# A fused scan and SwiGLU kernel on one core: the input projection of the scan moved next to the gate/up sums, its first loads reordered, its scan steps paced anew

## The chip, the cores and the metric

One core of a Trainium2 chip. The metric is device time in microseconds (us) of one execution. An execution over 1.5% above the fastest one of its kernel counts as slow. The mean granted TensorE clock of a run: 1.0 is full speed.

## The reference, cut to what matters

```python
xn = layernorm(x)                        # x: 2048 x 448, bf16
Bu = xn @ B_bar^T                        # complex, 448 states
h[t] = Lam_bar * h[t-1] + Bu[t]          # over 2048 steps
s  = 2 * Re(h @ C^T) + xn * Dskip
f  = (silu(xn @ w_gate) * (xn @ w_up)) @ w_down     # 448 -> 1792 -> 448
out = x + s * silu(f)
```

## The kernel before

The 2048 tokens are handled in four chunks (q = 0 to 3) of 512. For each chunk TensorE does: the gate/up sums (`gp`, `up`, fourteen tiles of 128 rows, two tiles at a time), the drive of the scan (`pb` six banks, `pk` one bank), the down projection (`hd`, four token tiles) and the output sums (`y`, four token tiles). VectorE turns the drive by a phase (six "E steps" into `ere`, `eim`), runs seven scans, turns back (six "H steps" into `H_re`, `H_im`), multiplies SiLU and up into `Vt`, and finishes each token tile (`t`, `ob`). ScalarE empties the gate/up and drive banks. The scan work is a queue of steps that other work lets through in portions; the budget is roughly VectorE us per call:

```python
def run(self, budget):                       # class Background
    self.credit = min(self.credit + budget, 2.0 * budget)
    while self.steps and self.credit > 0:
        _, cost, fn = self.steps.popleft()
        fn()
        self.credit -= cost
```

The gate/up and pb sums run as 64-row halves on both halves of the array. The second half of such a sum must not start before the first half of the other one is through, and that is told by a notice which passes through GpSimd:

```python
def tell(mm):
    told = nc.gpsimd.nop(nofuse=True)        # waits for mm; the other half waits for it
    tc.add_manual_dep(told.ins, mm.ins.name, SYNC, reason="share")
    return told.ins.name
```

The gate/up sums of a chunk, and what is hung between the pairs of tiles:

```python
def gu(q, bg, budget, hooks={}, begun=None):
    for f0 in range(0, NF, GRP):             # GRP = 4 tiles
        gs = work.tile([P, GRP, W], BF16, name="gs")
        us = work.tile([P, GRP, W], BF16, name="us")
        for i in range(0, n, 2):
            # ... banks gp, up; gu_matmuls; SiLU into gs, copy into us (ScalarE)
            for fn in hooks.get(fi // 2, ()):
                fn()
            bg.run(budget)
        nc.vector.tensor_tensor(out=Vt[...], in0=gs[...], in1=us[...], op=ALU.mult)
```

The order of chunks 1 to 3:

```python
bu_alloc(1)
gu(1, bg, 1.7, {
    0: [on(bu, 1, (0, 1, 2), True), on(bg.run, 5.0)],     # drive after the first pair
    1: [*stats(8, 9), on(ssm_steps, bg, 1)],
    # ... statistics and transposes of the next tokens, C weights
})
for q in range(NQ - 1):
    for j in range(TQ):
        sg.append(down(q, j))
        bg.run(2.2)
        if q + 2 < NQ and j == 1:
            bu(q + 2, (0, 1, 2), True)                    # drive inside the down projection
            bg.run(4.6)
    if q + 2 < NQ:
        ssm_steps(bg, q + 2)
    bg.finish(q)
    for j in range(TQ):
        finish(q, j, out_sum(q, j), sg[j])
    if q + 2 < NQ:
        gu(q + 2, bg, 1.7, {...})
# ... the last chunk
```

## Time and profile before

| | before |
|---|---|
| time, median of 3 runs | 196.47 us (195.99 to 199.16, the last one slow) |
| span of the profiled run, clock | 194.4 us, 0.999 |
| TensorE busy | 185.3 us |
| second tile pair of chunk 0 begins | 13.98 us |
| drive of chunk 1 (pb and pk) | 7.12 us |
| gate/up sums of chunk 2 / of chunk 3 | 23.3 / 21.3 us |

How to read it: TensorE's work sets the length, so what counts are the places where it stands still: the start, the drive of chunk 1, and the start of chunk 2's sums (2 us longer than the same sums of chunk 3). The prediction shows the lines.

### The profile page before, as it was taken

Reading aid. Unit: us, or ns where it says so; the run is one execution under the profiler, and the core shown is the slowest. Engines: PE = TensorE matmul, PEld = TensorE weight load, DVE = VectorE, ACT = ScalarE, POOL = GpSimd, SP = SyncE. Lnnn points to the kernel's source line nnn. Section 1 sums busy time; section 2 is a strip of 40 time slices with the busy share of each in tenths; the row PEclk is TensorE's granted clock in tenths of the full one; section 3 lists DMA queues with packets and bytes.
Section 4 is the critical chain, followed back from the end, with each engine's and each line's share of the span. In section 5 each row is a group of like instructions: output and inputs, shape, how many; then the busy total and the mean of one; then the engine's idle time right before and its main releaser. Section 6 shows DMA issues by size and latency. Waiting matters only on the chain.

```text
span 194.4 us, 3680 instructions
## 1 busy us (share of the span) xinstructions
PE 185.3 (95%) x1463; PEld 94.5 (49%) x1463; DVE 160.3 (82%) x265; ACT 104.3 (54%) x197; POOL 12.0 (6%) x21
## 2 busy tenths in 40 slices
PE   7889999998999999999799999999999999999991
PEld 3465434553444444554357854455444445555550
DVE  4589996799999999999999999998858789780063
ACT  3258699947999944910476751950476754102200
POOL 6322200000002000000003000000000000000000
PEclk9999999999999999999999999999999999999999
DMA  6999998300000240000200400001100000020002
GB/s 155 296 365 389 375 136 177 67 3 2 0 3 0 54 57 2 0 0 3 74 22 18 94 0 0 3 0 47 51 2 0 3 0 0 0 74 24 0 28 68
DMA packets 20977, 12.59 MB, mean 65 GB/s; under 512 B 10976, under 2 KB 19936, under 8 KB 20960
## 3 DMA queue, kind: packets, MB, share of 16 engines
q1 hardware_dynamic: 20544, 12.23, 25.1%
q8 instruction: 11, 0.18, 0.5%
q10 hardware_dynamic: 288, 0.13, 0.3%
q14 instruction: 6, 0.05, 0.1%
q0 software_dynamic: 128, 0.00, 0.0%
HBM read 8.03 MB, written 1.84 MB: 51 GB/s over the span
## 4 chain that ended last, share of the span: by engine, by line
PE 89%; DVE 4%; DMA 3%; SPq 1%; ACT 1%; issue 0%; POOL 0%; DVEq 0%
PE gp L428 23%; PE hd L564 22%; PE up L428 19%; PE y L578 11%; PE pb L428 10%; DMA x_all<-in_A_x_dram 3%; PE pk L451 2%; DVE t L591 2%; PE y L582 2%; DVE ob L593 1%; PE tpb L371 1%; DVE st L230 1%; SPq L144 0%; SPq L183 0%; ACT gs L551 0%
## 5 line engine op out<-in xcount | busy, mean ns | idle before, releaser
L428 PE MATMUL up<-xT,Wu 64*128 64x512 bf16 (+1 forms) x406 | 86.4, 369 | 1.6 <-DVE t L591 1.0
L428 PE MATMUL gp<-xT,Wg 64*128 64x512 bf16 (+1 forms) x406 | 87.0, 369 | 0.4 <-DVE t L591 0.4
L551 ACT ACTIVATE gs<-gp 128x512 bf16<-128x512 f32 x56 | 34.2, 611 | 33.6 <-PE gp L428 30.2
L428 PEld LDWEIGHTS <-Wg 64*128 64x128 bf16 x406 | 37.0, 94 | 24.0 <-issue 3.6
L428 PEld LDWEIGHTS <-Wu 64*128 64x128 bf16 x406 | 37.1, 94 | 19.5 <-POOLq L410 1.3
L564 PE MATMUL hd<-Wd,Vt 128*128 128x448 bf16 x224 | 43.4, 353 | 0.0
L552 ACT ACTIVATE us<-up 128x512 bf16<-128x512 f32 x56 | 34.5, 616 | 0.0
L564 PEld LDWEIGHTS <-Vt 128*128 128x128 bf16 x224 | 21.7, 98 | 21.3 <-issue 0.8
L569 ACT ACTIVATE sg<-hd 128x448 bf16<-128x448 f32 x16 | 8.7, 543 | 29.0 <-PE hd L564 29.0
L591 DVE TENSOR_TENSOR t<-y,sg 128x448 f32<-128x448 f32 x16 | 10.0, 624 | 15.1 <-PE y L578 14.7
L556 DVE TENSOR_TENSOR Vt<-gs,us 128x2048 bf16<-128x2048 bf16 (+1 forms) x16 | 17.3, 1084 | 5.5 <-ACT us L552 5.5
L428 PE MATMUL pb<-xT,BT 64*128 64x512 bf16 x168 | 19.9, 376 | 0.8 <-ACT gs L551 0.7
L578 PE MATMUL y<-C,H_re 128*128 128x448 bf16 x64 | 17.4, 353 | 0.0
L501 DVE TENSOR_TENSOR_SCAN bu_re<-rcol,H_re,ere 128x512 bf16<-128x512 f32 x12 | 15.0, 1266 | 0.0
L428 PEld LDWEIGHTS <-BT 64*128 64x128 bf16 x168 | 8.3, 94 | 11.4 <-issue 2.7
L582 PE MATMUL y<-Dd,xT 128*128 128x128 bf16 x64 | 13.6, 212 | 0.0
L230 DVE BATCH_NORM_STATS2 st<-x_all 128x6 f32<-128x448 bf16 x16 | 9.9, 619 | 3.3 <-DMA x_all<-in_A_x_dram 3.3
L215 POOL TENSOR_TENSOR sd<-vep,halves 128x1 bf16<-128x1 bf16 (+1 forms) x7 | 6.8, 972 | 85.2 <-DVE vep L232 83.2
L578 PE MATMUL y<-C,H_im 128*128 128x448 bf16 x48 | 11.7, 353 | 0.0
L501 DVE TENSOR_TENSOR_SCAN bu_im<-rcol,H_im,eim 128x512 bf16<-128x512 f32 x9 | 11.4, 1261 | 0.0
L463 ACT ACTIVATE bu_re<-pb 128x512 bf16<-128x512 f32 x12 | 7.3, 611 | 6.4 <-PE pb L428 6.4
L593 DVE TENSOR_TENSOR ob<-t,x_all 128x448 bf16<-128x448 f32 x16 | 10.0, 625 | 0.5
(95 smaller groups left out, 174.7 us busy)
## 6 DMA issues: line engine op xcount, KB each, us to landing
out_dram<-ob SPq DMA_DIRECT2D x16, 112.0 KB, 1.7
Wd<-in_B_w_down_dram SPq DMA_DIRECT2D x1, 1568.0 KB, 12.5
x_all<-in_A_x_dram SPq DMA_DIRECT2D x1, 896.0 KB, 14.5
Wg<-in_B_w_gate_dram SPq DMA_DIRECT2D x1, 768.0 KB, 8.2
Wu<-in_B_w_up_dram SPq DMA_DIRECT2D x1, 768.0 KB, 9.2
x_all<-in_A_x_dram SPq DMA_DIRECT2D x1, 448.0 KB, 6.1
Wg<-in_B_w_gate_dram SPq DMA_DIRECT2D x1, 384.0 KB, 6.7
Wu<-in_B_w_up_dram SPq DMA_DIRECT2D x1, 384.0 KB, 5.0
```

The source lines that it names most:

```text
L230: nc.vector.bn_stats(out=st[:], in_=x_all[:, n, :])
L428: mm = nc.tensor.matmul(banks[n][i][:, c0:c1], lhsT=weights[n][i][h, d, :], rhs=xT[h, d, q * W + c0 : q * W + c1], start=(first and m == 0 ...
L501: nc.vector.tensor_tensor_scan(out=T["b"][c][:, k, :], data0=rcol[:, k : k + 1].to_broadcast([P, W]), data1=T["e"][c][:, k, :], initial=in ...
L551: nc.scalar.activation(gs[:, i + j, :], gp_[:], ACT.Silu)
L552: nc.scalar.activation(us[:, i + j, :], up_[:], ACT.Copy)
L556: nc.vector.tensor_tensor(out=Vt[:, f0 : f0 + n, :], in0=gs[:, 0:n, :], in1=us[:, 0:n, :], op=ALU.mult)
L564: nc.tensor.matmul(hd, lhsT=Vt_of[q][:, fi, j * P : (j + 1) * P], rhs=Wd[:, fi, :], start=(fi == 0), stop=(fi == NF - 1),)
L569: nc.scalar.activation(sg[:], hd, ACT.Silu)
L578: nc.tensor.matmul(y, lhsT=h, rhs=C2[:, n, :], start=(n == 0), stop=(n == NS - 1))
L582: nc.tensor.matmul(y[:, s + c0 : s + P], lhsT=xT[:, n, m * P : (m + 1) * P], rhs=Dd[:, n, c0:P], start=False, stop=False,)
L591: nc.vector.tensor_tensor(out=t[:], in0=y, in1=sg[:], op=ALU.mult)
L593: nc.vector.tensor_tensor(out=ob[:], in0=t[:], in1=x_all[:, m, :], op=ALU.add)
```

## The change

The intent: the drive of each chunk becomes one piece beside the gate/up sums, so that TensorE has 5.5 us of other work exactly where it used to wait for banks; the scan steps are let through more slowly during the gate/up sums, so that the late work on VectorE does not stand ahead of `t`; at the start, token tiles 2 and 3 are loaded third, and the transposes of parameters move behind the first half sums.

```diff
-    load_w(nc.sync, nc.scalar, Wg, B_w_gate, 0, C0)
-    load_w(nc.sync, nc.scalar, Wu, B_w_up, 0, C0)
     load_x(2, TQ)
+    load_w(nc.sync, nc.sync, Wg, B_w_gate, 0, C0)
+    load_w(nc.scalar, nc.scalar, Wu, B_w_up, 0, C0)
...
-    nc.scalar.activation(pcol[:], params_row(), ACT.Copy)
-    warm(1)
+    warm(3)
     # statistics of tiles 2, 3; first half sums
...
+    nc.scalar.activation(pcol[:], params_row(), ACT.Copy)
     ln_transpose(2, nc.vector)
...
-    bu_alloc(1)
-    gu(1, bg, 1.7, {
-        0: [on(bu, 1, (0, 1, 2), True), on(bg.run, 5.0)],
-        1: [*stats(8, 9), on(ssm_steps, bg, 1)],
+    gu(1, bg, 0.9, {
+        1: stats(8, 9),
...
+    def drive(q, packed, budget):
+        bu_alloc(q)
+        bu(q, (0, 1, 2), packed)      # pk "first" or "last"
+        ssm_steps(bg, q)
+        bg.run(budget)
+
+    drive(1, "last", 4.8)
     for q in range(NQ - 1):
         for j in range(TQ):
             sg.append(down(q, j))
             bg.run(2.2)
-            if q + 2 < NQ and j == 1:
-                bu(q + 2, (0, 1, 2), True)
-                bg.run(4.6)
...
         if q + 2 < NQ:
+            drive(q + 2, "first", 4.0)
-            gu(q + 2, bg, 1.7, {...})
+            gu(q + 2, bg, 2.2 if last else 1.5, {...})
```

More of the change, by code (lines that the diff above doesn't have):

```diff
@@ L443, in sums, with bu @@
                 between()
-    def bu(q, ns, packed):
+    def bu(q, ns, packed=None):
+        pk = bank("pk") if packed == "first" else None
         pb = [[bank("pb") for _ in range(2)] for _ in ns]
-        pk = bank("pk") if packed else None
+        pk = bank("pk") if packed and pk is None else pk
         def whole():
@@ L456, in bu @@
         pairs = [[BT[:, :, block(n)], BT[:, :, block(KT + n)]] for n in ns]
-        alone = packed and len(ns) == 1
-        sums(pb, pairs, q, 0, W, between=whole if alone else None)
-        if packed and not alone:
+        if packed == "first":
+            whole()
+        sums(pb, pairs, q, 0, W, between=whole if packed == "between" else None)
+        if packed == "last":
             whole()
@@ L659 @@
         2: [*transposes(4, 5, 6, 7), on(load_c), on(table_phase, 1), on(table_sin, 1),
-            on(bu, 0, (0, 1), False), on(table_phase, 2), on(table_sin, 2)],
-        3: [on(bu, 0, (2,), True), on(table_phase, 3), on(table_sin, 3), on(params_fold)],
+            on(bu, 0, (0, 1)), on(table_phase, 2), on(table_sin, 2)],
+        3: [on(bu, 0, (2,), "between"), on(table_phase, 3), on(table_sin, 3), on(params_fold)],
         4: [on(params_trig), on(ssm_steps, bg, 0)],
@@ L673 @@
     })
+    def drive(q, packed, budget):
[4 more added lines that the diff above has]
+    drive(1, "last", 4.8)
     for q in range(NQ - 1):
         sg = []
-        if q + 2 < NQ:
-            bu_alloc(q + 2)
         for j in range(TQ):
@@ L680 @@
             bg.run(2.2)
-            if q + 2 < NQ and j == 1:
-                bu(q + 2, (0, 1, 2), True)
-                bg.run(4.6)
-        if q + 2 < NQ:
-            ssm_steps(bg, q + 2)
         bg.finish(q)
@@ L689 @@
         if q + 2 < NQ:
+            drive(q + 2, "first", 4.0)
             n = (q + 3) * TQ
-            gu(q + 2, bg, 1.7, {
+            last = q + 3 == NQ
+            gu(q + 2, bg, 2.2 if last else 1.5, {} if last else {
                 0: stats(n, n + 1),
@@ L696 @@
                 4: transposes(n + 2, n + 3),
-            } if q + 3 < NQ else {})
+            })
     q = NQ - 1
```

## The prediction

> **What bounds the kernel now.** I read the page's busy shares first, then the busy time by stretch, then the chain of waits around each stretch that fell short, then the order in time of VectorE and the DMA issues there.
>
> ```profile
> PE 185.3 (95%) x1463; PEld 94.5 (49%) x1463; DVE 160.3 (82%) x265; ACT 104.3 (54%) x197; POOL 12.0 (6%) x21
> ...
> PE 89%; DVE 4%; DMA 3%; SPq 1%; ACT 1%; issue 0%; POOL 0%; DVEq 0%
> ```
>
> TensorE is the bound: 185.3 us of 194.4, and 89% of the chain that ended last. A change that keeps its arithmetic can only win back its gaps. The columns below are stretch, length, then busy us and count of PE, PEld, DVE, ACT, POOL, then clock, DMA share, GB/s.
>
> ```profile
> 0.00:14.00 14.00, 11.34 (x109) 6.49 (x111) 8.70 (x34) 4.74 (x8) 5.65 (x17) 1.00 0.88 267
> ...
> 39.00:49.10 10.10, 9.30 (x79) 4.20 (x77) 9.86 (x19) 6.17 (x13) 0.00 (x0) 1.00 0.01 2
> ...
> 89.80:113.10 23.30, 21.86 (x197) 14.13 (x198) 22.38 (x41) 12.99 (x26) 1.92 (x1) 1.00 0.18 43
> ...
> 135.50:156.80 21.30, 21.30 (x198) 9.50 (x198) 16.20 (x16) 13.04 (x26) 0.00 (x0) 1.00 0.04 13
> ```
>
> The gate/up sums of chunk 2 take 23.3 us (89.8 to 113.1), the same sums of chunk 3 only 21.3 (135.5 to 156.8): 2.0 us lost. The other two losses are the start, and the 10 us after 39. The chain at the second:
>
> ```profile
> 42.32 1.74 PE pb L428 x16
> 44.06 0.02 issue
> 44.08 0.60 ACT gs L551
> 44.68 0.50 ACT us L552
> 45.18 0.04 issue
> 45.22 0.80 PE pb L428 x5
> ```
>
> TensorE runs the drive (pb) of chunk 1 after only one pair of gate/up tiles, needs PSUM banks that ScalarE has not emptied, and waits. The SiLU at 44.08 itself waits although its sums ended near 42: its buffer is freed by VectorE's product, which ran late (start, us):
>
> ```profile
> 42.77 1.22 DVE L556 TENSOR_TENSOR Vt<-gs,us 128x2048 bf16<-128x2048 bf16 x1
> ```
>
> At the third, TensorE waits for VectorE to read the y banks:
>
> ```profile
> 90.53 0.21 PE gp L428
> 90.77 0.63 DVE t L591
> 91.42 0.64 DVE ob L593
> ...
> 95.01 0.64 DVE t L591
> 95.69 0.37 PE up L428
> ```
>
> The first y was complete at about 85.2, but VectorE was still in the scan and the H products of chunk 1, queued ahead of t, until 90.8. At the start, token tiles 2 and 3 (issued at 2.66) land at 7.92, where the chain begins that ends in their transposes at 11.21; the weight tiles queued before them land sooner than their first user can run:
>
> ```profile
> 2.66 5.24 DMA x_all<-in_A_x_dram
> 7.92 0.64 DVE st L230
> ```
>
> **What the Trainium skill says.** "PSUM — Partial Sum Buffer", section Specifications (TRN2): eight banks of 2 KiB per partition. The trace agrees in effect: six pb, one pk and four gate/up banks are more than eight, and the waits at 44 and 95 are for banks. "TensorEngine Tiling (Array Packing)", section Key Properties: changing the tiling mode drains the engine. Here gate/up and pb run as 64-row halves, and pk, hd, y use all 128 rows. The first 28 hd matmuls after gate/up take 5.40 us, the next run of 28 takes 5.30; four pk after pb take 0.97 against 4 x 0.216 = 0.86; gp after y takes 0.32 against 0.21. So a switch costs about 0.105 us. "DMA: Bandwidth & Descriptors", section Queues, rings and completion order: each engine consumes a ring's descriptors in order, though completions need not be. The trace agrees loosely: x of tiles 2 and 3 lands after the weights issued before it.
>
> **The change, part by part.** No multiply or scan is added; two 0.2 us warm-up matmuls are. I built the changed kernel and read its order and waits, then did sums with durations of the trace of before.
>
> Start. Tiles 2 and 3 are now third in the ring, the gate weights behind them, the up weights on ScalarE's queue. Before, the third transfer (192 KB) landed at 4.8 and the fourth at 5.8; with 224 KB third and 128 KB more beside it I expect x near 5.3 and the last gate weights near 7.1. Both tiles of tokens 0 and 1 leave ScalarE at 7.3, so the first half sums begin at 7.4 instead of 7.88, and run with a wait of about 0.2 us for GpSimd's notice instead of 0.4 + 0.7: end 9.2 instead of 10.4. The parameter transposes (0.36) now follow: 9.6. Two token transposes: 10.4; sixteen B transposes (B lands near 9.2): 11.4; second half sums (1.55): 12.95 instead of 13.98. The next tile needs the second part of the up weights, which landed at 12.9 and 13.3 before and may be issued earlier by half a microsecond now. Taken: 13.0, gain 1.0. It survives to chunk 1, as the ScalarE row that is full from 24.5 to 40.9 starts when VectorE's phase tables are ready, and VectorE (running without a break from 12.0) starts 1.2 earlier.
>
> Drive of chunk 1. From the start of gate/up of chunk 1 (38.9) the drive no longer follows the first pair. That pair's SiLU still waits for the late product, some 1.6 to 2.1 us after its sums, but the next pair has its own banks (3.02 us of work), so the wait is covered or costs 0.2 at most. Before, pb and pk took 41.96 to 49.08 = 7.12; in one piece they take 42 matmuls in pairs of 0.216 = 4.53, pk 0.86, two switches 0.21: 5.60. Gain 1.5, less 0.1.
>
> Finishing chunk 0. I count TensorE from T, the start of gate/up of chunk 1: gate/up 7 x 3.02 = 21.2, drive(1) 5.5, down 10.6, y 6.1. So the y sums begin at T+37.3 and the first y is complete at T+38.8. VectorE: the last product of chunk 1 comes at about T+28 (it must trail ScalarE by 2 us and has scans, statistics and C weights in front), six H steps (3 x 0.87 + 3 x 1.14 = 6.0) end at T+34: the y sums find H ready with 3 us to spare. Then six E steps (6.0) and one scan (1.2) end at T+41, so t of the first y is 2.5 us late, and four t/ob pairs at 1.3 end at T+46.4. But TensorE now goes from y (end T+43.4) into the drive of chunk 2 for 5.5 us, whose fourth bank is the first that waits for a t, at T+45.2 against T+42. Gate/up of chunk 2 starts at T+48.9 and needs the last t by T+46. The 2.06 us (23.33 less 21.27) go.
>
> Switches. Before, chunks 2 and 3 had hd-pb-pk-hd-y-gp and gp-hd; now y-pk-pb-gp-hd, two fewer each; chunk 1 loses two also. 6 x 0.105 = 0.6.
>
> Sum: 1.0 + 1.4 + 2.0 + 0.6 = 5.0 us, which I take as 4.9 as the stretches leave a few tenths unexplained; the tail after the last y (190.2 to 194.4) stays. 196.47 - 4.9 = 191.6.
>
> **The rivals.** First: the banks of pk. In drives 2 and 3 pk is summed first but emptied last by ScalarE (0.48 per pb copy, then pk and two half copies). In the trace the last half copy ends 8.1 us after pb begins, so 9.1 after the new drive begins. If the first gate/up tiles needed that bank, at 5.5, each drive would stall 3.6 us: 7 us, and the kernel would take 199. The built program has the fourth bank of the second pair wait for it, at 5.5 + 3.0 + 0.9 = 9.4: a margin of only 0.3, against which a stall of a few tenths is possible.
>
> Second: VectorE as the new bound. It is 82% busy and has the same work in fewer us. For: it has no idle time from 35 to 130. Against: its spare time now lies where products wait for ScalarE, and by my count H of chunk 1 is ready at T+71 for T+81, H of chunk 2 before T+108 for T+124. If the paced scans put the products of chunk 1 later than I count by over 3 us, y of chunk 0 would wait; 1 to 3 us, time 193 to 195.
>
> Third: the start is bound by transfers (DMA share about 1.0 from 8 to 25 us), and moving x forward merely delays weights. Then its 1.0 is 0 to 0.4, time 192.3.
>
> **Range and chances.** If the start fails the gain is 3.9, if everything holds and the second weights come early it is 5.5; a stall from the first or second rival takes off 1 to 3. I predict 191.6, with 190.5 to 193.3 for 8 in 10. Faster by over 2% means below 192.5, four fifths of the way to my sum: 0.70. Within 2%: 0.28. Slower: 0.02.
>
> **What would show it.** Right: no wait of TensorE on t; gate/up of chunk 2 in 21.3 us; no SiLU on the chain inside a drive; pb and pk near 5.5 in each; the second tile pair of chunk 0 starting near 13.0. Wrong: TensorE idle on a bu copy in the second pair of chunk 2 or 3 (first rival), on H_re before the first y (second), or the first half sums starting at 7.9 with a weight transfer as releaser (third).

## The result, and the profile after

The changed kernel takes 190.74 us (median of 4 runs, 190.62 to 191.12); the kernel before took 196.83 (median of 4, 195.99 to 199.16). The 199.16 is slow, 1.6% above the fastest; the other three have a median of 196.47, 5.7 above the changed kernel. The ratio of the fast runs is 0.9708, interval 0.9667 to 0.9749. Ratios here are the mean time of one kernel's fast runs over that of the other's of the same rounds, so not quite the ratio of the medians quoted. The profiled runs have spans of 194.4 and 188.8 us, both at a clock of 0.999 or 1.0.

The page after: busy us of the engines, and the shares of the chain that ended last.

```profile
PE 182.8 (97%) x1465; PEld 92.5 (49%) x1465; DVE 160.0 (85%) x265; ACT 104.0 (55%) x197; POOL 10.9 (6%) x21
...
PE 94%; DVE 2%; DMA 1%; ACT 0%; POOL 0%; issue 0%; DVEq 0%
```

TensorE now holds 94% of the chain, where it held 89%. The busy time by stretch after (columns as in the prediction): the start, the gate/up sums of chunk 1, its drive, and the gate/up sums of chunk 2.

```profile
0.00:12.20 12.20, 10.34 (x109) 6.60 (x111) 8.41 (x33) 4.68 (x8) 5.59 (x17) 1.00 0.89 279
...
37.20:59.00 21.80, 21.80 (x204) 11.55 (x200) 21.23 (x45) 18.60 (x38) 1.40 (x1) 1.00 0.07 14
59.00:64.50 5.50, 5.50 (x48) 2.81 (x45) 5.46 (x9) 4.19 (x9) 0.00 (x0) 1.00 0.24 48
...
86.60:107.80 21.20, 21.20 (x199) 9.42 (x194) 20.11 (x35) 17.71 (x35) 1.03 (x1) 1.00 0.16 26
```

In every stretch after the start TensorE is busy throughout. The chain of waits after, at the drives of chunks 1 and 2, has nothing between their pieces:

```profile
58.97 4.53 PE pb L428 x42
63.50 0.97 PE pk L453 x4
...
81.15 0.86 PE pk L453 x4
82.01 4.64 PE pb L428 x42
```

5.50 us each. VectorE's order in time (start, us) at the finish of chunk 0, before: seven scans and three H products of chunk 1 stand ahead of the first `t`.

```profile
79.66 2.45 DVE L501 TENSOR_TENSOR_SCAN bu_re<-rcol,H_re,ere 128x512 bf16<-128x512 f32 x2
...
86.73 1.26 DVE L501 TENSOR_TENSOR_SCAN bu_im<-rcol,H_im,eim 128x512 bf16<-128x512 f32 x1
...
89.89 0.96 DVE L495 TENSOR_TENSOR H_im<-H_im,tmp 128x1536 bf16<-128x1536 bf16 x1
90.77 0.62 DVE L591 TENSOR_TENSOR t<-y,sg 128x448 f32<-128x448 f32 x1
```

After: one scan stands ahead of the first `t`, and the fourth `t` ends at 84.51, while drive 2 runs (81.15 to 86.65).

```profile
78.47 1.28 DVE L504 TENSOR_TENSOR_SCAN bu_re<-rcol,H_re,ere 128x512 bf16<-128x512 f32 x1
79.67 0.60 DVE L594 TENSOR_TENSOR t<-y,sg 128x448 f32<-128x448 f32 x1
...
83.89 0.62 DVE L594 TENSOR_TENSOR t<-y,sg 128x448 f32<-128x448 f32 x1
```

The issues of the DMA queue at the start, after (start, us). Token tiles 2 and 3 go out at 1.66, before at 2.66; the second up weights at 6.41 and 6.89, before at 7.91 and 8.33:

```profile
1.66 0.43 SPq L138 DMA_DIRECT2D x_all<-in_A_x_dram  x1
...
6.41 0.43 SPq L144 DMA_DIRECT2D Wu<-in_B_w_up_dram  x1
6.89 0.48 SPq L148 DMA_DIRECT2D Wu<-in_B_w_up_dram  x1
```

The first matmul of full width (64x512), which opens the second tile pair, in TensorE's order in time, before:

```profile
13.98 0.38 PE L428 MATMUL up<-xT,Wu 64*128 64x512 bf16 x1
```

and after:

```profile
12.23 0.38 PE L428 MATMUL up<-xT,Wu 64*128 64x512 bf16 x1
```

Laid side by side, the two traces give this account of the 5.6 us of span (boundaries read off TensorE's order):

| stretch | before, us | after, us | gain |
|---|---|---|---|
| to the second tile pair | 13.98 | 12.23 | 1.75 |
| from there to gate/up of chunk 1 | 25.12 | 25.24 | -0.12 |
| gate/up and drive of chunk 1 | 28.29 | 27.00 | 1.29 |
| down, y (and drive 2) of chunk 0 | 22.39 | 22.18 | 0.21 |
| gate/up of chunk 2 | 23.33 | 21.15 | 2.18 |
| down, y (and drive 3) of chunk 1 | 22.39 | 22.28 | 0.11 |
| gate/up of chunk 3 | 21.26 | 21.16 | 0.10 |

These sum to 5.52.

### The profile page after: what moved, and what is told of

The parts are those of the page before. It is cut to its first block, busy times and chain, and to the rows that moved or that the text cites. A ratio compares the mean times of both kernels' runs of the same rounds, so it can differ in the third digit from the quotient of the medians.

```text
span 188.8 us, 3686 instructions
## 1 busy us (share of the span) xinstructions
PE 182.8 (97%) x1465; PEld 92.5 (49%) x1465; DVE 160.0 (85%) x265; ACT 104.0 (55%) x197; POOL 10.9 (6%) x21
## 4 chain that ended last, share of the span: by engine, by line
PE 94%; DVE 2%; DMA 1%; ACT 0%; POOL 0%; issue 0%; DVEq 0%
PE gp L428 24%; PE hd L567 23%; PE up L428 21%; PE y L581 11%; PE pb L428 10%; PE pk L453 2%; PE y L585 2%; DMA x_all<-in_A_x_dram 1%; PE tpb L371 1%; DVE st L230 1%; PE tp L259 1%; DVE t L594 0%; DVE ob L596 0%; ACT xT L261 0%; POOL sd L215 0%; DVE xn L248 0%
## 5 line engine op out<-in xcount | busy, mean ns | idle before, releaser
L554 ACT ACTIVATE gs<-gp 128x512 bf16<-128x512 f32 x56 | 35.0, 626 | 10.9 <-PE gp L428 7.4
L555 ACT ACTIVATE us<-up 128x512 bf16<-128x512 f32 x56 | 35.4, 632 | 0.0
L428 PE MATMUL pb<-xT,BT 64*128 64x512 bf16 x168 | 19.2, 376 | 0.0
L215 POOL TENSOR_TENSOR sd<-vep,halves 128x1 bf16<-128x1 bf16 (+1 forms) x7 | 5.7, 814 | 77.2 <-PE up L428 41.8
```

The costliest lines, as they stand in the source:

```text
L428: mm = nc.tensor.matmul(banks[n][i][:, c0:c1], lhsT=weights[n][i][h, d, :], rhs=xT[h, d, q * W + c0 : q * W + c1], start=(first and m == 0 ...
L554: nc.scalar.activation(gs[:, i + j, :], gp_[:], ACT.Silu)
L555: nc.scalar.activation(us[:, i + j, :], up_[:], ACT.Copy)
```

## The experiments

Twelve kernels ran, four to a session on one chip, six times each, beside eleven runs of the kernel before in each session: its medians were 196.97, 196.99 and 196.44 in the three sessions. All twelve were correct.

**Taking the change apart.** *The whole start alone*, in the kernel before:

```diff
 load order, warm(3) and parameter transposes as in the change; all else as before
```

> The start alone: loads reordered and the parameter transposes moved, everything else as before. My theory (each part of the gain stands in its own stretch, and the start is worth the 1.75 us by which the second tile pair of chunk 0 now begins earlier, 12.23 against 13.98): 1.7 us faster than before, about 194.8 us. Rival (the start is swallowed later, as the first chunk ends on ScalarE and VectorE): under 0.5 us.

Measured: 194.91 (194.86 to 195.15), ratio 0.9891 (0.9856 to 0.9927). The second tile pair begins at 12.51 and the later waits (0.7 for the SiLU, 1.0 and 0.4 for `t`) are all there. Against the five runs of before at 0.994 or more in the same rounds (median 196.61) that is 1.7 us: the start is worth what was expected of it at this point, more than the 1.0 of the prediction.

*All but the start*, in the changed kernel:

```diff
-    load_x(2, TQ)
-    load_w(nc.sync, nc.sync, Wg, B_w_gate, 0, C0)
-    load_w(nc.scalar, nc.scalar, Wu, B_w_up, 0, C0)
+    (the order of before), and the parameter transposes with warm(1) in front again
```

> The drives moved and the scans paced anew, with the start as before. My theory: 3.8 to 4.1 us faster than before, about 192.5 us, so that this and the start alone add up to the whole 5.7. Rival (the moves only pay because the start comes earlier): under 3 us.

Measured: 193.01 (191.69 to 193.41), ratio 0.9783 (0.9744 to 0.9822). The size is about right, but the scatter of 1.7 us is not, in a kernel whose later stages have no waits left. Its waits of TensorE (us in total, times, longest):

```profile
PE tv L279 <- DMA vrow<-in_A_Dskip_dram: 1.7, 1, 1.7
```

The transposes of the parameters (tv) wait for the last parameter load, and the first half sums stand behind them in TensorE's order. The transposes begin at 8.24 here and at 7.22 in the profile of before.

*Only the load order*, and *only the parameter transposes*, each in the kernel before:

> Only the load order of the start: token tiles 2 and 3 third, up weights on the other queue; parameter transposes where they were. My theory (the early tokens are what counts): first half sums still begin at 7.9 behind the parameter transposes but run without a wait, second tile pair near 12.5, gain 1.3 to 1.6 us. Rival (the parameter transposes, waiting for their load until 7.2, held the start): under 0.5 us.

> Only the parameter transposes moved behind the first half sums, with three warm-up matmuls; loads as before. My theory: the half sums begin at 7.2 but then wait for the statistics of tiles 2 and 3, which land at 7.9 as before: gain 0 to 0.3 us. Rival: 1 us or more.

Load order alone: 195.89, ratio 0.9939 (0.9892 to 0.9985), in two groups: 194.79 to 195.19 at a clock of 0.999 or 1.0, and 196.59 to 196.86 at 0.991. The gain is there in the first group (194.91 in its middle, 1.7 below the 196.61 of before at 0.994 or more in the same rounds, where 1.3 to 1.6 was expected), and is not in the second. Its profile has the second tile pair at 12.71. The transposes alone: 196.52, ratio 0.9978 (0.9942 to 1.0015), the same, as expected. So the new load order makes the gain of the start; moving the transposes adds little at the same clock. But it does something for the clock: five of its six runs, and all six of the whole start, were at 0.995 or more, against five of eleven of the kernel before in the same rounds.

**What goes with the groups: the clock.** The Trainium skill, page "TensorE: Matmul & The Clock Gate", Part 1, says that TensorE's clock is gated to half when it has been idle for a window of about 3.4 us, and that the window runs freely. The busy time by stretch of the run without the start part (last three columns: clock, DMA share, GB/s; the first count is TensorE's):

```profile
7.00:8.00 1.00, 0.00 (x0) 0.00 (x0) 0.00 (x0) 0.19 (x1) 0.00 (x0) 1.00 0.99 304
8.00:9.00 1.00, 0.76 (x7) 0.48 (x7) 0.57 (x1) 0.19 (x1) 0.00 (x0) 0.67 1.09 381
9.00:10.00 1.00, 1.00 (x11) 0.64 (x12) 0.93 (x4) 0.00 (x0) 0.46 (x1) 0.50 1.15 355
10.00:11.00 1.00, 1.00 (x12) 0.72 (x10) 0.80 (x4) 0.00 (x0) 0.61 (x2) 0.50 0.90 287
11.00:12.00 1.00, 1.00 (x14) 0.61 (x8) 0.56 (x2) 0.00 (x0) 0.03 (x1) 0.62 1.06 367
```

TensorE stood still for 1.7 us, then worked at half clock. A clock of 0.67 over a us means 0.66 us at half, 0.62 means 0.76: with the two between, 3.42 us at half clock, which costs 1.71 us of dense work, and takes the mean clock of a 195 us run to 1 - 1.71/195 = 0.991, the value of the slower group of the load order alone, which was not profiled itself. (A mean of 0.995 need not cost anything: in the profiles of the whole start and of *pk last* below it comes from half clock after the last matmul.) To test it, the idle time of this kernel was filled with warm-up matmuls, with the transposes left where they were:

```diff
+    warm(6)
     nc.scalar.activation(pcol[:], params_row(), ACT.Copy)
     warm(1)
```

> The changed kernel with the start of before, as once run (median 193.01, 191.69 to 193.41, with clocks of 0.986 to 0.999), plus six warm-up matmuls in front of the parameter transposes, which fill TensorE's idle time there (1.7 us in the profile of that run, followed by 3.3 us at a granted clock of 0.5). Theory (the half clock follows the idle time, and explains the scatter): all runs at a clock of 0.994 or more, scatter below 0.8 us, median 191.7 to 192.3. Rival (the clock dips by themselves): the same scatter and the same clocks of 0.986 to 0.991 in some runs, median near 193.2.

Measured: 191.79 (191.51 to 191.93), all six at a clock of 0.999 or 1.0. The same stretches in its profile:

```profile
7.00:8.00 1.00, 1.00 (x10) 0.50 (x8) 0.55 (x1) 0.23 (x1) 0.00 (x0) 1.00 0.89 278
8.00:9.00 1.00, 1.00 (x16) 0.72 (x16) 0.93 (x4) 0.19 (x1) 0.43 (x1) 1.00 1.09 369
9.00:10.00 1.00, 1.00 (x21) 0.62 (x16) 0.82 (x5) 0.00 (x0) 0.62 (x2) 1.00 1.07 368
```

The rival, that the clock dips by itself, falls: six useless matmuls take away the dips and most of the scatter, and bring all runs to where only the two undisturbed ones of the kernel without them were (191.69 and 192.29); the median is 1.2 us lower, though from another session (in which the kernel before still fell to 0.986 to 0.991 in five of its eleven runs). With the clock out of the way the changed kernel is 191.79 less 190.74, 1.05 us, faster. That is less than the whole start is worth, since the second tile pair comes at 13.50 in this profile and at 13.98 in that of before, which also waits 0.4 for GpSimd's notice.

*Early x without the new queues*, in the changed kernel:

```diff
     load_x(2, TQ)
-    load_w(nc.sync, nc.sync, Wg, B_w_gate, 0, C0)
-    load_w(nc.scalar, nc.scalar, Wu, B_w_up, 0, C0)
+    load_w(nc.sync, nc.scalar, Wg, B_w_gate, 0, C0)
+    load_w(nc.sync, nc.scalar, Wu, B_w_up, 0, C0)
```

> The changed kernel, but with the weights of the start spread over the two queues as before (both first parts on SyncE's queue, both small parts on ScalarE's); token tiles 2 and 3 stay third. Theory A (the start gains because x comes earlier and SyncE's issues no longer stop for it): within 0.3 us of the changed kernel, 190.6 to 191.1, second tile pair of chunk 0 at 12.1 to 12.5. Rival (it gains because the up weights sit on a second queue): 0.7 us or more slower, 191.4 to 192, second tile pair near 13.

Measured: 190.68 (five runs within 190.66 to 190.68, and the profiled one at 191.12), ratio 0.9716 (0.9683 to 0.9750). The time is that of the changed kernel, so the rival, the second queue for the weights, falls: it is worth nothing measurable. The place of the second tile pair missed the expectation, 12.97 in the profile, but that is the slowest of the six runs, in which TensorE waited 0.8 us for a normalised tile; the faster five were not looked into.

**The drives and the pace.** *pk last in all drives*, in the changed kernel:

```diff
-            drive(q + 2, "first", 4.0)
+            drive(q + 2, "last", 4.0)
```

> The changed kernel with pk summed last instead of first in the drives of chunks 2 and 3. Two more switches between half-row and full-row matmuls in each of two drives. Theory of the switches (0.105 us each): 0.4 us slower than the changed kernel, about 191.2 us. Theory that pk goes first for its bank's sake: a wait in the second gate/up pair, over 1 us slower, or a gain. If a switch costs nothing: the same within 0.1.

Measured: 191.24 (191.11 to 191.30), ratio 0.9709 (0.9680 to 0.9739), 0.5 slower than the changed kernel, which ran in other rounds. The chain shows a switch of the tiling mode before and after pb (pk takes 0.97 us here, 0.86 above where y, of the same mode, precedes it):

```profile
81.30 4.64 PE pb L428 x42
85.94 0.97 PE pk L453 x4
```

*Only drive 1 moved*: drives 2 and 3 back inside the down projection and the later sums back at their old pace of 1.7, with the pace of the sums of chunk 1 still at 0.9.

```diff
-            drive(q + 2, "first", 4.0)      # behind the finish of q
+            bu(q + 2, (0, 1, 2), "last"); bg.run(4.6)      # behind down(q, 1), as before
```

> The changed kernel, but the drives of chunks 2 and 3 back between the second and third down projection. Before the first t of chunk 0 stand 5 scans and no H product of chunk 1, against 1 scan in the changed kernel and 7 scans with 3 H products before. By my count t of the last y of chunk 0 is done near 89.2 and is needed at 90.7. Theory (what cost the 2 us was VectorE's queue ahead of t, not the place of the drive): 0.3 to 0.6 us slower than the changed kernel, for the switches, about 191.3. Rival (the drive's place removed the wait): 2 us slower, about 192.8.

Measured: 191.15 (191.09 to 191.37), ratio 0.9708 (0.9678 to 0.9738), no wait of TensorE on `t`. So it is not the place of drives 2 and 3 beside the finish that removes the 2 us; 0.4 is what is left for them and the later pace (across rounds), the size of the four switches.

*Only drives 2 and 3 moved*: drive 1 back behind the first pair, with its old pace.

```diff
-    gu(1, bg, 0.9, {
-        1: stats(8, 9),
+    bu_alloc(1)
+    gu(1, bg, 1.7, {
+        0: [on(bu, 1, (0, 1, 2), "last"), on(bg.run, 5.0)],
+        1: [*stats(8, 9), on(ssm_steps, bg, 1)],
...
-    drive(1, "last", 4.8)
```

> The changed kernel, but the drive of chunk 1 back behind the first gate/up pair, with the old pace of chunk 1. Six scans of chunk 1 then stand before the first t of chunk 0, near 85.2, while the moved drive of chunk 2 needs it at 84.2 and the third t (88.6) at 85. Theory (move and pace hang together): the 1.3 us of the first drive are lost and the drive of chunk 2 waits some 3.5 us for t: 4 to 5 us slower than the changed kernel, 195 to 196 us. Rival (each part stands by itself): 1.3 to 1.5 us slower, 192.2.

Measured: 198.00 (196.20 to 199.03), ratio 1.0036 (0.9979 to 1.0093): the whole gain is gone, and more than was expected. Six scans stand ahead of the first `t`, which comes at 85.61. TensorE's waits in its profile:

```profile
PE pb L428 <- DVE t L594: 2.6, 3, 1.2
...
PE pb L428 <- ACT gs L554: 0.7, 1, 0.7
```

And behind the waits on `t` the half clock again (stretches as above):

```profile
88.00:89.00 1.00, 0.00 (x0) 0.00 (x0) 0.83 (x3) 0.00 (x0) 0.00 (x0) 1.00 0.03 8
89.00:90.00 1.00, 0.99 (x8) 0.54 (x9) 0.87 (x2) 0.00 (x0) 0.00 (x0) 0.73 0.36 115
90.00:91.00 1.00, 1.00 (x8) 0.37 (x5) 0.97 (x3) 0.00 (x0) 0.00 (x0) 0.50 0.33 115
91.00:92.00 1.00, 1.00 (x8) 0.41 (x6) 1.00 (x2) 0.24 (x1) 0.00 (x0) 0.50 0.20 56
92.00:93.00 1.00, 1.00 (x8) 0.48 (x6) 0.97 (x2) 0.85 (x2) 0.00 (x0) 0.56 0.29 85
```

0.54 + 2 + 0.88 is 3.42 us at half clock once more. That is most of the miss: the two runs at 0.995 or more took 196.2 and 196.3, just above the range expected, the other four, at 0.983 to 0.989, 197.8 to 199.0. The move of drives 2 and 3 without the new pace only puts pb where gate/up stood waiting.

*The old pace everywhere*, with all drives moved:

```diff
-    gu(1, bg, 0.9, {
+    gu(1, bg, 1.7, {
...
-            gu(q + 2, bg, 2.2 if last else 1.5, {...})
+            gu(q + 2, bg, 1.7, {...})
```

> The changed kernel with the old budgets per gate/up pair (1.7 everywhere). Chunk 0 is done earlier and five scans of chunk 1, instead of one, stand before the first t: 4.7 us later, near 84.4, where the drive of chunk 2 wants it at 82.9 and the third t at 83.7 against 87.8. Theory (the pace is needed): 3 to 4 us slower than the changed kernel, 194 to 195 us. Rival (the pace is decoration, since VectorE has the time): within 0.3 us.

Measured: 194.93 (194.78 to 195.69), ratio 0.9907 (0.9874 to 0.9940), as expected in total and in the number of scans (five) ahead of the first `t`. But the trace does not put it down to `t` alone. TensorE's order in time has two waits (the idle time and its releaser in brackets):

```profile
53.59 0.39 PE L428 MATMUL up<-xT,Wu 64*128 64x512 bf16 x1 [1.92 <-POOLq L410]
...
87.56 2.96 PE L428 MATMUL pb<-xT,BT 64*128 64x512 bf16 x25 [0.64 <-DVE t L594]
```

The larger one is at GpSimd's notice between the halves of a gate/up sum. Though it is longer than the wait of 1.7 us at the start above, no half clock followed it here (third column from the end):

```profile
52.00:53.00 1.00, 0.00 (x0) 0.00 (x0) 0.93 (x4) 0.61 (x2) 0.00 (x0) 1.00 0.00 0
...
54.00:55.00 1.00, 1.00 (x12) 0.49 (x10) 1.00 (x3) 0.55 (x2) 0.96 (x1) 1.00 0.09 16
```

GpSimd's order in time says why TensorE waits:

```profile
53.55 1.41 POOL L215 TENSOR_TENSOR sd<-vep,halves 128x4 bf16<-128x4 bf16 x1 [33.74 <-DVE vep L232]
```

A square root stands ahead of the notice in GpSimd's queue, and its input, the variance (vep), is made by VectorE behind the additional scans. TensorE goes on at 53.59, 0.04 after the square root starts and long before its 1.41 us are over: what held the notice was the late input. In the changed kernel the same instruction comes at 51.40, about when the notice is needed. The two waits are 2.6 of the 4.2 us by which this kernel is slower than the changed one. In TensorE's order the pb sums of drive 1 take 0.7 more (5.36 against 4.65) and the sums of chunk 2 0.4 more (21.67 against 21.25), which was not followed up. So the pace does two things: it brings `t` forward, and it keeps the statistics from stopping TensorE through GpSimd. Neither the prediction nor this expectation had the second.

*The pace alone, with nothing moved*: the kernel before, with the scans of chunk 1 held back.

```diff
-    gu(1, bg, 1.7, {
-        0: [on(bu, 1, (0, 1, 2), True), on(bg.run, 5.0)],
+    gu(1, bg, 1.2, {
+        0: [on(bu, 1, (0, 1, 2), True)],
```

> The kernel before with one thing new: scans of chunk 1 are held back, only two stand before the first t (seven, and six H products, before). Drive places, start and order of pk are those of before. Theory (VectorE's queue ahead of t causes the 2.06 us): no wait of TensorE on t at the start of chunk 2's sums, 1.8 to 2.2 us faster than before, 194.7 to 195.2; the wait of the drive of chunk 1 for the SiLU (0.7) stays. Rival (the place of the drive causes it): no gain, 196.5 to 197.

Measured: 194.17 (193.52 to 194.83), ratio 0.9892 (0.9852 to 0.9932). The three runs at 0.997 or more took 193.5 to 193.7, those of before at 0.995 or more in the same rounds 195.4 to 196.4. VectorE's order:

```profile
84.04 2.46 DVE L501 TENSOR_TENSOR_SCAN bu_re<-rcol,H_re,ere 128x512 bf16<-128x512 f32 x2
86.41 0.60 DVE L591 TENSOR_TENSOR t<-y,sg 128x448 f32<-128x448 f32 x1
...
90.64 0.62 DVE L591 TENSOR_TENSOR t<-y,sg 128x448 f32<-128x448 f32 x1
```

The waits on `t` are gone, with every drive where it was. (The expectation speaks of six H products ahead of `t` before; the trace above has three.) This settles the third loss: it was VectorE's queue, and the two edited lines recover it. The waits that are left are those of the start and of drive 1:

```profile
PE tv L279 <- DMA vrow<-in_A_Dskip_dram: 1.1, 1, 1.1
PE pb L428 <- ACT gs L551: 0.7, 1, 0.7
```

**A version that beats both.** In the changed kernel the first SiLU of chunk 1 still waits for its buffer, which a late product on VectorE (41.14 to 42.36) frees, though the view names the last matmul; ScalarE's order in time:

```profile
42.45 0.60 ACT L554 ACTIVATE gs<-gp 128x512 bf16<-128x512 f32 x1 [3.15 <-PE up L428]
```

With a slower pace in chunk 0 the product stands three steps earlier in VectorE's queue, and begins at 38.28:

```diff
-    gu(0, bg, 2.0, {
+    gu(0, bg, 1.2, {
```

> The changed kernel with the scan steps in chunk 0's gate/up stage paced at 1.2 instead of 2.0, so that the third product of chunk 0 stands two VectorE steps earlier and the first SiLU of chunk 1 need not wait for its buffer. If that late product is what makes gate/up of chunk 1 take 21.8 us (37.2 to 59.0) where chunks 2 and 3 take 21.2: 0.3 to 0.6 us faster than the changed kernel, 190.1 to 190.5. If it is another cost (a switch, transposes and C weights between the sums): no gain, 190.6 to 190.9. If H of chunk 0 now comes too late: slower by its wait.

```profile
40.07 0.60 ACT L554 ACTIVATE gs<-gp 128x512 bf16<-128x512 f32 x1 [0.78 <-PE gp L428]
```

The SiLU comes 2.4 us earlier, and the time is 190.53 (190.45 to 190.65), ratio 0.9706 (0.9673 to 0.9739): 0.2 better than the changed kernel, less than the 0.3 to 0.6 expected. Drive 1 begins at 58.81 instead of 58.97, so the trace agrees. The 0.6 that was to be won had been read from stretch boundaries that were 0.27 too early (the sums of chunk 1 begin at 37.47, not at 37.2); the true excess was 21.50 less 21.15, 0.35. The difference of 0.2 is between kernels of different rounds, but no run of this kernel was as slow as the median of the changed one, 190.74, and in the same rounds the variant with early x on the old queues, as fast as the changed kernel, had 190.68.

## Why the prediction was right

The time lay within the range, 0.9 below the 191.6 predicted and 0.2 above the low end. By its own steps:

**Start, 1.0 predicted.** Right in mechanism, too small: 1.75 in the traces. The terms that were mis-sized are two: the first half sums ended at 8.86 instead of 9.2 (they began at 7.22 instead of 7.4 and had no wait for GpSimd's notice at all), and the two token transposes after them took 0.46 (9.24 to 9.70) instead of the 0.8 put down. The second up weights, feared as a limit at 13.0, were there at 12.3. That the first up weights now have another queue was not the reason for the time: with the old queues it is the same. The third rival, a start bound by transfers, is refuted by the loads alone.

**Drive of chunk 1, 1.5 less 0.1.** 1.29 in the traces. The drive takes 5.50 (5.60 predicted, which counts two switches where the trace has one, before pk). The late product did what was said of it, "covered or costs 0.2 at most": the last experiment won 0.2 by taking it away.

**Finish of chunk 0, 2.06.** 2.18, a switch of about 0.1 among it. The cause given, scans and H products ahead of `t`, is shown by the experiment that changed only that and got 2.1 (193.63 against 195.73, medians of the runs at 0.994 or more). But the prediction spoke as if the 5.5 us of drive 2 were needed to cover a `t` that is 2.5 us late; with drives 2 and 3 in their old places `t` was not waited for either. What was needed was the pace: without it drive 2 at its new place waited 2.6 us for `t`. So this term came out right in size, with the cause right and its cover wrong.

**Switches, 0.6.** Seen at 0.11 (0.97 against 0.86 for pk, 4.64 against 4.53 for pb), and the stretches around the down projections and chunk 3 gained 0.42 together. Undoing two of them in each of drives 2 and 3 cost 0.5, where 4 x 0.105 is 0.42.

**The rivals.** The bank of pk, with its margin of 0.3 us, was not waited for: the sums of chunk 2 took 21.15. H of chunk 0 ended at 72.2, long before y. VectorE is busier (85%) but still not the bound; where the pace is wrong it becomes one, through GpSimd.

**What was missed.** The clock. Over the three sessions 14 of the 33 runs of before had a clock of 0.994 or more; within each session their median was 0.8 to 1.2 below that of the others. The changed kernel's four runs were all at 0.996 or more. How much of the measured 5.7 this makes is not shown: of the runs of before beside them only the profiled one has its clock on record (0.999), and it is already 5.6 longer in span than the profiled run after. That the wait at the parameter transposes is what triggers the half clock in the kernel before was only argued from its variants: no profile of before caught it. Nor does a low mean always cost time: with the old pace everywhere the runs at 0.986 to 0.991 took 194.85 to 195.50, those at 0.996 or more 194.78 to 195.69.

## What to carry to other kernels

When an engine that is not the bound holds up the one that is, look at the order of its queue before moving work on the bound engine: here two lines of pacing gave the 2 us, and the pace was also what the move of the drives needed. A wait of TensorE can cost more than its length: the 3.42 us of half clock behind one are worth up to 1.71 us of work, by the estimate above, though not every wait is followed by it (one of 1.92 us kept the full clock). Filling a wait that can't be removed with idle matmuls is worth trying. And a notice through an idle-looking engine can be held by an operation ahead of it in that engine's queue whose input is late.

## What the Trainium skill lacked or had wrong

- "TensorE: Matmul & The Clock Gate", Part 1 puts the half clock "after ≥1 idle window (~3.4µs)". Here it followed waits of 1.7 us and 1.1 us at the start, and 2.6 us in three pieces, the longest 1.2, in another kernel: less idle time at a stretch than one window. (Further on in Part 1, in "A second HAM failure mode: psum-queue depth-cycling", the page itself tells of short, frequent idle times that were enough in another kernel.) The length of the half clock, 3.42 us in each of the two profiles shown, agrees with the page. The page gives no share of idle time that is enough, and the runs don't fix one: the kernel before idles 1.3 us of two at 94 to 96 in its profile and kept its clock, and so did the old pace everywhere behind a wait of 1.92 us.
- "TensorEngine Tiling (Array Packing)", Key Properties says that a change of tiling mode drains the engine, without a cost: 0.11 us per switch here (pk 0.97 against 0.86), and 0.5 us in 191 for four, measured across rounds.
- No page that I found gives a figure for what a notice through GpSimd's queue can cost when an operation with a late input stands ahead of it: 1.92 us here.
